# Eight second operands behind the weights of two MLP groups, and row sums that begin later: an FNet and MLP-Mixer kernel on one core

## The chip, the core and the metric

The kernel runs on one NeuronCore of a Trainium2 chip. The core has five engines with an instruction stream each. TensorE (PE in the profile) multiplies; its weight loads are shown as PEld. VectorE (DVE) does arithmetic on whole tiles, ScalarE (ACT) copies and activations, GpSimd (POOL) and SyncE (SP) mostly issue transfers here. Each engine works through its instructions strictly in the order in which they were written, and waits where an instruction needs something that another engine or a transfer has not finished. The metric is the device time of one execution, in microseconds; less is better.

## The reference

```python
def reference(A_x, A_dft_seq_re, A_dft_seq_im, A_dft_hid_re, A_dft_hid_im, B_x, B_w1, B_b1, B_w2, B_b2):
    x = A_x                                   # 1 x 2048 x 512, float32
    xn = _layernorm(x, axis=-1)
    # A: a = xn @ hid_re.T, b = xn @ hid_im.T   (2048 x 512)
    #    s = seq_re @ a - seq_im @ b                 (2048 x 2048 times 2048 x 512)
    s = _A_ref(xn, A_dft_seq_re, A_dft_seq_im, A_dft_hid_re, A_dft_hid_im)
    # B: y = layernorm(xn); h = gelu(y @ w1 + b1)  (2048 x 1792); h @ w2 + b2
    g = _silu(_B_ref(xn, B_w1, B_b1, B_w2, B_b2))
    return x + s * g
```

All inputs and the output are float32.

## The kernel before

Each float32 matrix product is made of three matmuls in a rounded format: an operand is split into a high part (ScalarE copies it rounded, `w1_round`, `y_round`, `a_round`) and a low part (VectorE subtracts the high part from the original, `w1_rest`, `y_rest`, `a_rest`), and high times high, high times low and low times high are added up in PSUM. On top of that the large products use a seven-product scheme for 2 x 2 blocks (Strassen's, in Winograd's form): sums of blocks are made first, seven block products follow instead of eight, and sums of the products give the result. So VectorE has to make, for every product, the sums as well as the low parts.

The program has four stages, each one long run of matmuls on TensorE.

1. **Hidden DFT, first half of the tokens** (`dft_mm`, line 338).
2. **Hidden DFT, second half** (`q_product`, `q_mm`, line 537): seven products in the order 1, 2, 5, 6, 3, 7, 4, each in four chunks c of six matmuls. Products 1, 6, 7 and 4 add into the same four PSUM banks one after the other. After product 6 ScalarE reads each bank (`q_after`, line 520), after product 7 VectorE reads it (line 525), and only then may product 4 add its own chunk to that bank.
3. **MLP, first layer** (`h_product`, line 657): seven groups j of weight columns, for each of them seven products in the order 1, 5, 6, 2, 3, 7, 4 (product 4 of one group comes after product 5 of the next). For groups 0 and 1 the tokens are taken in two halves (s): group 0 with the second half (`ONE`), group 1 with the second half, group 0 with the first half (`ZERO`), group 1 with the first half. A product of one half is six matmuls, of both halves twelve. The right operands are the normalised tokens and their sums: `11`, `t1`, `t2`, `21`, `22`, `t3`, `t4` for products 1, 5, 6, 2, 3, 7, 4, each once per half (in the profile `y_0h`, `yt_0l` and so on: a digit for the half, 0 is the first, then h or l for the part; a t marks the sums). `y_scale` (line 461) multiplies by the row of factors, `y_sum` (line 475) makes the sums in place. The left operands are the weights of the group: `w1_load` (line 433) fetches 512 KB, `w1_sums` (lines 437 to 440) makes four sums, `w1_round` (line 444) and `w1_rest` (line 83) split them. The weights have a single raw buffer, so the next load waits for `w1_rest` of the group before; the loads of groups 1 and 2 are issued by GpSimd, the others by SyncE. `h_after` moves products out of PSUM: ScalarE copies or applies GELU (lines 673 and 662), VectorE adds product 2 (line 702), product 3 (line 708) and product 7 (line 712). Product 4 adds into the bank that line 712 reads, so TensorE has to wait for line 712 before it.
4. **MLP, second layer** (`m_product`, line 838; products in the order 1, 4, 2, 5, 6, 3, 7 with seven units j each), and then the **sequence DFT** (line 838 too, then line 1156). In each unit of the second layer VectorE and ScalarE prepare operands three units ahead; SyncE loads them five ahead into seven buffers of a pool called `room`.

The sequence DFT needs sums of the hidden DFT's results. They are made by eight pieces of work, `extras[0]` to `extras[7]` (function `sums_a`), each in three steps: load two tiles of 512 KB (line 733), four VectorE operations (lines 737 to 740), store four results of 256 KB (line 744). Before the change pieces 0 to 4 run in groups 1 to 5 of the first layer and pieces 5, 6, 7 in products 5, 6 and 3 of the second layer. Their tiles come from the same `room` pool.

The order of all this is written out by hand: a table of `then(...)` steps that run between the chunks of `q_product`, and a table `y_late` of steps that run before a given product of the first layer. The order in the tables is the order in which VectorE and ScalarE get their instructions.

## Time and profile before

| what | value |
|---|---|
| time, median of 3 runs (lowest, highest) | 682.1 us (680.96, 682.46) |
| the profiled execution: its own time | 681.11 us |
| the profiled execution: span from first to last instruction | 679.3 us |
| TensorE busy | 664.6 us, 2908 matmuls |
| VectorE busy | 544.2 us, 592 instructions |
| ScalarE busy | 354.3 us, 395 instructions |
| moved by DMA | 172.28 MB, mean 254 GB/s |

The profile comes from one execution. Times inside it count from the span's start. A row of a timeline has the start, the duration, the engine, the line, the operation, the tiles written and read, how many instructions are merged into the row, and in brackets how long the engine was idle before it and what ended that. Instructions of one engine overlap a little, so the step from one start to the next is often shorter than the duration. A matmul of this kernel takes 0.39 us from start to end, while the next one starts 0.227 us later when nothing holds it up.

### The profile page before, as it was taken

To read this page: it belongs to the slowest core of one execution; us is meant where nothing else is said; L and a number is where in the kernel's file an instruction comes from. 1 tells how busy PE (TensorE), PEld (TensorE's weight loads), DVE (VectorE), ACT (ScalarE), POOL (GpSimd) and SP (SyncE) were. 2 spreads that over 40 slices of the span, in tenths; PEclk is the share of its full clock that TensorE was granted. 3 is DMA by queue.
4 is the path that set the end of the run, shared out by engine and by line. 5 is a ranking of instruction groups with operands and counts; after the bars stand their busy time and mean duration, and the time that the engine had idled before them with its cause. 6 is when DMAs were issued, how large, how long until landed. Compare 5 with 4: busy or idle time off the path is not lost.

```text
span 679.3 us, 8185 instructions
## 1 busy us (share of the span) xinstructions
PE 664.6 (98%) x2908; PEld 543.2 (80%) x2908; DVE 544.2 (80%) x592; ACT 354.3 (52%) x395; POOL 50.6 (7%) x84
## 2 busy tenths in 40 slices
PE   8999987999999999999999999999999999999997
PEld 5887875877888888888888888888888888888885
DVE  7998986487887775777997998729977389998985
ACT  4745664544445746656365654537445364646540
POOL 1001000122212110000000100000000001220100
PEclk9999998999999999999999999999999999999999
DMA  9778270398999998588899998415544548997983
GB/s 318 258 270 216 102 247 32 144 334 322 381 357 313 402 419 335 192 276 305 306 317 410 394 324 302 147 57 187 185 156 119 161 109 250 304 254 244 308 263 126
DMA packets 70329, 172.28 MB, mean 254 GB/s; under 512 B 6640, under 2 KB 21008, under 8 KB 70288
## 3 DMA queue, kind: packets, MB, share of 16 engines
q1 hardware_dynamic: 57904, 131.36, 54.8%
q0 software_dynamic: 12032, 39.86, 18.9%
q10 hardware_dynamic: 352, 0.54, 0.2%
q8 instruction: 23, 0.38, 0.2%
q14 instruction: 18, 0.15, 0.1%
HBM read 121.38 MB, written 50.35 MB: 253 GB/s over the span
## 4 chain that ended last, share of the span: by engine, by line
PE 84%; DVE 5%; issue 5%; DMA 2%; ACT 2%; POOL 1%; SPq 0%; POOLq 0%; DVEq 0%; ACTq 0%
PE pz L838 19%; PE px L838 18%; PE ma L838 11%; PE mb L838 8%; PE hy L657 8%; PE pd L338 6%; PE pw L838 5%; PE hz L657 3%; PE hx L657 2%; PE px L1156 2%; PE pw L1156 2%; POOL h_d L665 1%; DMA rw<-wt 1%; DVE xT L475 1%; DVE q L525 1%
## 5 line engine op out<-in xcount | busy, mean ns | idle before, releaser
L944 DVE TENSOR_TENSOR c<-c,c 128x1024 f32<-128x1024 f32 x32 | 39.0, 1220 | 4.1 <-DMA c<-ct 4.1
L662 ACT ACTIVATE hc<-hc,b_t 128x1024 f32<-128x1024 f32 (+1 forms) x18 | 17.3, 962 | 26.6 <-DVE hc L702 22.4
L65 DVE TENSOR_TENSOR R_b1l<-c,R_b1h 128x1024 fp32r<-128x1024 f32 x16 | 19.5, 1221 | 14.0 <-ACT R_b1h L64 10.7
L838 PE MATMUL pw<-R_s1h,L 128*128 128x512 f32 x96 | 29.7, 389 | 0.0
L64 ACT ACTIVATE R_s3h<-c 128x1024 fp32r<-128x1024 f32 x16 | 17.0, 1061 | 23.8 <-DVE c L944 12.4
L64 ACT ACTIVATE R_b2h<-c 128x1024 fp32r<-128x1024 f32 x16 | 16.9, 1058 | 21.6 <-DVE c L949 17.1
L65 DVE TENSOR_TENSOR R_s2l<-c,R_s2h 128x1024 fp32r<-128x1024 f32 x16 | 19.5, 1222 | 8.9 <-PE pz L838 8.9
L64 ACT ACTIVATE R_s2h<-c 128x1024 fp32r<-128x1024 f32 x16 | 17.0, 1061 | 16.7 <-PE px L838 9.3
L83 DVE TENSOR_TENSOR w1l<-w1r,w1h 128x1792 fp32r<-128x1792 f32 x7 | 14.2, 2023 | 13.1 <-ACT w1h L444 13.1
L65 DVE TENSOR_TENSOR R_s3l<-c,R_s3h 128x1024 fp32r<-128x1024 f32 x16 | 19.5, 1221 | 3.9 <-PE pz L838 3.8
L64 ACT ACTIVATE R_s1h<-c 128x1024 fp32r<-128x1024 f32 x16 | 16.4, 1051 | 11.6 <-DVE c L955 11.6
L64 ACT ACTIVATE R_b1h<-c 128x1024 fp32r<-128x1024 f32 x16 | 16.7, 1053 | 11.1 <-DMA c<-ct 5.1
L952 POOL DMA_DIRECT2D c<-ct x8 | 7.0, 875 | 201.5 <-issue 148.1
L64 ACT ACTIVATE R_a1h<-c 128x1024 fp32r<-128x1024 f32 x16 | 16.9, 1054 | 8.9 <-PE pz L838 7.2
L657 PE MATMUL hy<-yt_1h,w1h 128*128 128x512 f32 x42 | 17.1, 408 | 4.3 <-DVE hc L712 4.3
L838 PEld LDWEIGHTS pw<-R_s1h,L 128*128 128x128 f32 x96 | 18.0, 188 | 3.7
L65 DVE TENSOR_TENSOR R_b2l<-c,R_b2h 128x1024 fp32r<-128x1024 f32 x16 | 19.4, 1219 | 1.5 <-PE px L838 1.5
L65 DVE TENSOR_TENSOR R_a1l<-c,R_a1h 128x1024 fp32r<-128x1024 f32 x16 | 19.5, 1220 | 1.0 <-PE px L838 0.7
L65 DVE TENSOR_TENSOR R_s4l<-c,R_s4h 128x1024 fp32r<-128x1024 f32 x16 | 19.5, 1220 | 0.7 <-PE px L838 0.7
L64 ACT ACTIVATE w2h<-w 128x1024 fp32r<-128x1024 f32 (+1 forms) x14 | 13.2, 946 | 12.8 <-DVE w L770 3.9
L949 DVE TENSOR_TENSOR c<-c,c 128x1024 f32<-128x1024 f32 x16 | 19.6, 1223 | 0.4
L64 ACT ACTIVATE R_s4h<-c 128x1024 fp32r<-128x1024 f32 x16 | 16.8, 1052 | 5.3 <-PE pz L838 4.9
(950 smaller groups left out, 2221.9 us busy)
## 6 DMA issues: line engine op xcount, KB each, us to landing
c<-ct SPq DMA_DIRECT2D x68, 512.0 KB, 6.1
m<-h_d SPq DMA_DIRECT2D x48, 512.0 KB, 6.6
h_d<-ht POOLq DMA_DIRECT2D x21, 512.0 KB, 6.6
s_d<-sa SPq DMA_DIRECT2D x32, 256.0 KB, 4.0
la<-s_d SPq DMA_DIRECT2D x32, 256.0 KB, 6.2
h_d<-hc POOLq DMA_DIRECT2D x13, 512.0 KB, 4.8
x<-x SPq DMA_DIRECT2D x16, 256.0 KB, 4.9
sa<-a_d SPq DMA_DIRECT2D x8, 512.0 KB, 5.6
```

The costliest lines, as they stand in the source:

```text
L64: nc.scalar.activation(hi, src, AF.Copy)
L65: nc.vector.tensor_sub(lo, src, hi.bitcast(F32))
L83: nc.vector.tensor_sub(hi_lo[1], src, hi_lo[0].bitcast(F32))
L338: nc.tensor.matmul(acc, xt[i, k][px], weights[m * NK + k][pw], start=n == 0, stop=n == len(terms) - 1)
L475: nc.vector.tensor_sub(t, y_raw[a, tau], y_raw[b, tau])
L657: nc.tensor.matmul(acc[:, tau, :], w[:, W1_AT[p], k * P:(k + 1) * P], r[:, k, :], start=p in (1, 5, 2) and i == 0, stop=p in (2, 3, 4) and ...
L662: nc.scalar.activation(dst, src, AF.Gelu_apprx_tanh, bias=b1_t[:, row:row + 1])
L838: nc.tensor.matmul(acc[k][:, tau, :], a, c[:, tau, :], start=first and i == 0, stop=last and i == len(terms) - 1, skip_group_check=True)
L944: nc.vector.tensor_sub(t, t, raw)
L949: nc.vector.tensor_add(raw, raw, t)
L952: nc.gpsimd.dma_start(out=t, in_=ct[1, 1, n], accum_op=ALU.add)
L1156: nc.tensor.matmul(acc[KEY[name]][k][:, tau, :], a[k], c[:, tau, :], start=False, stop=u == us[-1] and i == 2, skip_group_check=True)
```

## The change

Three things move; no operation is added or removed, and no size changes.

In the second half of the hidden DFT and in groups 0 and 1 of the first layer, the steps of `w1` (sums, rounding, low parts and loads of groups 0 and 1) are written further ahead, and the steps that make the right operands of the first token half are written later: `11` and `t1` come behind the weights of group 0, `t2`, `21`, `22`, `t3` and `t4` are spread over both half groups of the second token half, and the end of `t4` falls into group 0's first token half. `w1_sums(2)` goes into the same table. The table `y_late` gets the token half as part of its key. Pieces 0 to 2 of the row sums run in groups 3 to 5, and pieces 3 and 4 in products 4 and 2 of the second layer.

```diff
--- before.py
+++ after.py
@@ -603,9 +603,9 @@
     a_rest(5)
     y_rest("t1", 1)
     q_product(1, [then(y_scale, 1, 3), then(y_round, "22", 1)], [then(y_sum, "t2", 1)],
-              [then(y_round, "t2", 1), then(y_rest, "22", 1)], [then(y_rest, "t2", 1), then(a_round, 6)])
-    q_product(2, [post(2, 0), then(a_rest, 6)], [post(2, 1), then(y_sum, "t3", 1)],
-              [post(2, 2), then(y_round, "t3", 1), then(a_round, 3)], [post(2, 3)])
+              [then(y_round, "t2", 1), then(y_rest, "22", 1)], [then(a_round, 6)])
+    q_product(2, [post(2, 0), then(y_rest, "t2", 1)], [post(2, 1), then(a_rest, 6)],
+              [post(2, 2), then(y_sum, "t3", 1), then(y_round, "t3", 1), then(a_round, 3)], [post(2, 3)])
     q_product(5, [then(a_rest, 3)], [then(y_rest, "t3", 1), then(y_sum, "t4", 1), then(a_round, 7)],
               [then(y_round, "t4", 1), then(a_rest, 7)], [then(y_rest, "t4", 1)])
     early.close()
@@ -613,14 +613,12 @@
     wp = early.enter_context(tc.tile_pool(name="wp", bufs=4, reuse_waits="tile"))
     lp = early.enter_context(tc.tile_pool(name="lpm", bufs=2, reuse_waits="tile"))
     w1_load(0)
-    q_product(6, [then(y_scale, 0, 0), then(y_round, "11", 0)], [then(y_scale, 0, 1)],
-              [then(y_rest, "11", 0), then(y_sum, "t1", 0)], [then(y_round, "t1", 0)])
-    q_product(3, [post(3, 0), then(y_rest, "t1", 0)], [post(3, 1), then(w1_sums, 0)], [then(w1_round, 0), post(3, 2)],
-              [post(3, 3)])
-    q_product(7, [post(7, 0)], [post(7, 1), then(w1_rest, 0), then(w1_load, 1)], [post(7, 2)],
-              [post(7, 3), then(y_scale, 1, 1)])
-    q_product(4, [then(y_sum, "t2", 0), then(y_round, "t2", 0)], [then(y_rest, "t2", 0)], [then(w1_sums, 1)],
-              [then(y_scale, 1, 0)])
+    q_product(6, [then(y_scale, 0, 0)], [then(w1_sums, 0)], [then(w1_round, 0), then(y_scale, 0, 1)], [then(w1_rest, 0), then(w1_load, 1)])
+    q_product(3, [post(3, 0), then(y_round, "11", 0)], [post(3, 1), then(y_scale, 1, 1)], [post(3, 2), then(y_rest, "11", 0)],
+              [post(3, 3), then(y_sum, "t1", 0)])
+    q_product(7, [post(7, 0), then(y_round, "t1", 0)], [post(7, 1), then(w1_sums, 1)], [post(7, 2), then(y_rest, "t1", 0)],
+              [post(7, 3), then(w1_round, 1)])
+    q_product(4, [then(w1_rest, 1), then(w1_load, 2)], [then(y_sum, "t2", 0)], [], [then(y_scale, 1, 0)])
 
     rows_ps.close()
     yp = ctx.enter_context(tc.tile_pool(name="yp", bufs=4, space=bass.MemoryType.PSUM, reuse_waits="tile"))
@@ -791,12 +789,17 @@
         h_seq += [(j, p, s, done) for p in (1, 5)] + ([(last[0], 4, last[1], None)] if last else [])
         h_seq += [(j, p, s, done) for p in (6, 2, 3, 7)]
         last = j, s
-    y_late = {(0, 5): [then(w1_round, 1)],
-              (0, 6): [then(y_round, "21", 0), then(y_rest, "21", 0), then(w1_rest, 1), then(w1_load, 2)],
-              (0, 2): [then(y_round, "22", 0)],
-              (0, 3): [then(y_rest, "22", 0), then(y_sum, "t3", 0), then(y_round, "t3", 0)],
-              (0, 7): [then(y_rest, "t3", 0), then(y_sum, "t4", 0)],
-              (1, 1): [then(y_round, "t4", 0), then(y_rest, "t4", 0)]}
+    y_late = {(0, 5, 1): [then(y_round, "t2", 0)],
+              (0, 6, 1): [then(y_rest, "t2", 0)],
+              (0, 3, 1): [then(y_round, "21", 0)],
+              (0, 7, 1): [then(y_rest, "21", 0)],
+              (1, 5, 1): [then(y_round, "22", 0)],
+              (1, 6, 1): [then(y_rest, "22", 0), then(y_sum, "t3", 0)],
+              (1, 2, 1): [then(y_round, "t3", 0)],
+              (1, 3, 1): [then(y_rest, "t3", 0), then(w1_sums, 2)],
+              (1, 7, 1): [then(y_sum, "t4", 0)],
+              (0, 5, 0): [then(y_round, "t4", 0)],
+              (0, 6, 0): [then(y_rest, "t4", 0)]}
 
 
     m_order = [1, 4, 2, 5, 6, 3, 7]
@@ -995,7 +998,7 @@
             w2_load(1, 1)
 
     for j, p, s, done in h_seq:
-        for o in y_late.get((j, p), ()) if s == ONE else ():
+        for o in y_late.get((j, p, s.start), ()):
             o()
         h_product(j, p, s)
         if j == NJ - 1:
@@ -1009,12 +1012,13 @@
         if stores:
             store()
         if p == 4 and s.start == 0 and j + 2 < NJ:
-            w1_sums(j + 2)
+            if j:
+                w1_sums(j + 2)
             w1_split(j + 2)
             if j + 3 < NJ:
                 w1_load(j + 3)
-        if 0 < j < NJ - 1 and s.start == 0 and p in (1, 2, 3):
-            extras[j - 1][{1: 0, 2: 1, 3: 2}[p]]()
+        if 2 < j < NJ - 1 and p in (1, 2, 3):
+            extras[j - 3][{1: 0, 2: 1, 3: 2}[p]]()
 
     for u, (p, j) in enumerate(m_units):
         m_ahead("load", u + (6 if u < 2 else 5))
@@ -1053,8 +1057,8 @@
                 w2_split(nxt, 1)
         if j == 1 and p in (4, 2):
             w2_load(0, 1) if p == 4 else w2_load(1, 0)
-        if p in (5, 6, 3) and j in (0, 2, 4):
-            extras[{5: 5, 6: 6, 3: 7}[p]][j // 2]()
+        if p in (4, 2, 5, 6, 3) and j in (0, 2, 4):
+            extras[{4: 3, 2: 4, 5: 5, 6: 6, 3: 7}[p]][j // 2]()
         if (p, j) == (7, NJ - 1):
             m_evacuate(7)
         if p == 7:
```

Three places show what that does to the order. First VectorE at the end of the hidden DFT. `q5_` with `qy` are its reads after product 7 (line 525), `w1r0` and `w1r1` the raw weights of groups 0 and 1. Before:

```order
L525 SCALAR_TENSOR_TENSOR q5_0_792<-qy0_694,nq_89,q5_0_792 128x512
L525 SCALAR_TENSOR_TENSOR q5_0_792<-qy1_707,nq_89,q5_0_792 128x512
L83 TENSOR_TENSOR w1l0_911<-w1r0_841,w1h0_910 128x1792
L525 SCALAR_TENSOR_TENSOR q5_2_815<-qy2_716,nq_89,q5_2_815 128x512
L525 SCALAR_TENSOR_TENSOR q5_2_815<-qy3_729,nq_89,q5_2_815 128x512
L461 TENSOR_TENSOR xT1_1_237<-xT1_1_237,rowR_0_674 128x1024
L475 TENSOR_TENSOR xT0_0_676<-xT1_1_237,xT0_0_676 128x1024
L83 TENSOR_TENSOR yt2_0l_970<-xT0_0_676,yt2_0h_969 128x1024
L437 TENSOR_TENSOR w1r1_940<-w1r1_940 128x256
L438 TENSOR_TENSOR w1r1_940<-w1r1_940 128x256
L439 TENSOR_TENSOR w1r1_940<-w1r1_940 128x256
L440 TENSOR_TENSOR w1r1_940<-w1r1_940 128x256
```

And now:

```order
L83 TENSOR_TENSOR w1l0_872<-w1r0_841,w1h0_871 128x1792
L525 SCALAR_TENSOR_TENSOR q6_0_849<-qz0_785,qq_88,q6_0_849 128x512
L525 SCALAR_TENSOR_TENSOR q6_0_849<-qz1_795,qq_88,q6_0_849 128x512
L461 TENSOR_TENSOR xT1_1_237<-xT1_1_237,rowR_0_674 128x1024
L525 SCALAR_TENSOR_TENSOR q6_2_869<-qz2_808,qq_88,q6_2_869 128x512
L83 TENSOR_TENSOR y11_0l_894<-xT0_0_676,y11_0h_893 128x1024
L525 SCALAR_TENSOR_TENSOR q6_2_869<-qz3_821,qq_88,q6_2_869 128x512
L475 TENSOR_TENSOR xT0_0_676<-xT1_0_235,xT0_0_676 128x1024
L525 SCALAR_TENSOR_TENSOR q5_0_792<-qy0_694,nq_89,q5_0_792 128x512
L525 SCALAR_TENSOR_TENSOR q5_0_792<-qy1_707,nq_89,q5_0_792 128x512
L437 TENSOR_TENSOR w1r1_883<-w1r1_883 128x256
L438 TENSOR_TENSOR w1r1_883<-w1r1_883 128x256
```

The low part of group 0's weights now stands in front of the last reads after product 3 and of all reads after product 7, and the first two operands of the first token half (`y11_0`, `yt1_0`) stand between them; the sum `t2` is behind them.

Second VectorE in the first two half groups of the first layer. `hc50` and `hc51` are where the results of product 7 go for groups 0 and 1 (line 712 before, 710 now). Before, up to group 0's:

```order
L83 TENSOR_TENSOR y21_0l_1080<-xT0_1_680,y21_0h_1079 128x1024
L83 TENSOR_TENSOR w1l1_1067<-w1r1_940,w1h1_1066 128x1792
L702 TENSOR_TENSOR hc10_1063<-hc10_1063,hx0_1098 128x512
L83 TENSOR_TENSOR y22_0l_1096<-xT1_1_237,y22_0h_1095 128x1024
L475 TENSOR_TENSOR xT1_0_235<-xT1_1_237,xT1_0_235 128x1024
L708 TENSOR_TENSOR hu20_1092<-hu20_1092,hz0_1069 128x512
L83 TENSOR_TENSOR yt3_0l_1111<-xT1_0_235,yt3_0h_1110 128x1024
L475 TENSOR_TENSOR xT0_0_676<-xT0_1_680,xT0_0_676 128x1024
L712 TENSOR_TENSOR hc50_1076<-hc50_1076,hy0_1056 128x512
```

Now, up to group 0's, and then up to group 1's:

```order
L461 TENSOR_TENSOR xT0_1_680<-xT0_1_680,rowR_0_674 128x1024
L83 TENSOR_TENSOR yt2_0l_1069<-xT0_0_676,yt2_0h_1068 128x1024
L700 TENSOR_TENSOR hc10_1065<-hc10_1065,hx0_1091 128x512
L706 TENSOR_TENSOR hu20_1088<-hu20_1088,hz0_1071 128x512
L83 TENSOR_TENSOR y21_0l_1102<-xT0_1_680,y21_0h_1101 128x1024
L710 TENSOR_TENSOR hc50_1078<-hc50_1078,hy0_1058 128x512
```

```order
L700 TENSOR_TENSOR hc11_1128<-hc11_1128,hx1_1163 128x512
L83 TENSOR_TENSOR yt3_0l_1161<-xT1_0_235,yt3_0h_1160 128x1024
L437 TENSOR_TENSOR w1r2_976<-w1r2_976 128x256
L438 TENSOR_TENSOR w1r2_976<-w1r2_976 128x256
L439 TENSOR_TENSOR w1r2_976<-w1r2_976 128x256
L440 TENSOR_TENSOR w1r2_976<-w1r2_976 128x256
L706 TENSOR_TENSOR hu21_1158<-hu21_1158,hz1_1133 128x512
L475 TENSOR_TENSOR xT0_0_676<-xT0_1_680,xT0_0_676 128x1024
L710 TENSOR_TENSOR hc51_1140<-hc51_1140,hy1_1121 128x512
```

Before, four operations on operands (`y22_0l`, two sums, `yt3_0l`) stand between line 702 and line 712 beside line 708; now one does between lines 700 and 710, `y21_0l`, beside line 706. Ahead of group 1's line 710 there are now a low part, the four weight sums of group 2 and a sum, which before were done earlier or, for the weight sums, later.

Third SyncE in the second layer, ahead of the loads of the weights `w221`, which the sum for product 5 needs in product 2 (line 770). `m16` and its like are operands of that layer, `sa` the tiles of the row sums, `s1_d3` and its like the stored results of piece 3. Before:

```order
L812 DMA m16_2301<-h2_d2_1016 128x1024
L812 DMA m17_2323<-h2_d3_1017 128x1024
L812 DMA m18_2341<-h2_d4_1018 128x1024
L812 DMA m19_2363<-h2_d5_1019 128x1024
L763 DMA w221_0_2383<-w2 128x1024
L763 DMA w221_1_2384<-w2 128x768
```

And now:

```order
L742 DMA s1_d3_144<-sa1_3_2199 256x1x256
L742 DMA s3_d3_160<-sa0_3_2197 256x1x256
L742 DMA s2_d3_152<-sa0_3_2197 256x1x256
L742 DMA s4_d3_168<-sa1_3_2199 256x1x256
L815 DMA m16_2289<-h2_d2_1018 128x1024
L815 DMA m17_2311<-h2_d3_1019 128x1024
L815 DMA m18_2329<-h2_d4_1020 128x1024
L731 DMA sa0_4_2351<-a_d4_129 128x2x512
L731 DMA sa1_4_2353<-b_d4_137 128x2x512
L815 DMA m19_2355<-h2_d5_1021 128x1024
L761 DMA w221_0_2375<-w2 128x1024
L761 DMA w221_1_2376<-w2 128x768
```

The four stores of piece 3 and both loads of piece 4 are now in front of these weights; in product 4 the loads of piece 3 stand in the same way in front of the weights `w212` for product 2.

## The prediction

> **What bounds the kernel now.** I read the page's head first, then who TensorE waits for, then TensorE's timeline around its waits.
>
> ```profile
> span 679.3 us, 8185 instructions
> PE 664.6 (98%) x2908; PEld 543.2 (80%) x2908; DVE 544.2 (80%) x592; ACT 354.3 (52%) x395; POOL 50.6 (7%) x84
> ...
> PE hy L657 <- DVE hc L712: 5.7, 3, 4.3
> PE hy L657 <- ACT q L520: 1.8, 1, 1.8
> ```
>
> TensorE is busy 98% of the span, so only its gaps can be won. By far the largest two lie at the first layer: three waits for VectorE's line 712, 5.7 us together and 4.3 us the longest, and one of 1.8 us for ScalarE's reads after product 4 of the hidden DFT. TensorE's timeline shows where, and what follows:
>
> ```profile
> 92.12 0.39 PE L537 MATMUL qy<-W,yt_1l 128*128 128x512 f32 x1
> 94.27 0.50 PE L657 MATMUL hy<-y_1h,w1h 128*128 128x512 f32 x1 [1.76 <-ACT q L520]
> ...
> 105.07 0.39 PE L657 MATMUL hz<-yt_1h,w1l 128*128 128x512 f32 x1
> 109.78 0.70 PE L657 MATMUL hy<-yt_1h,w1h 128*128 128x512 f32 x1 [4.32 <-DVE hc L712]
> ...
> 114.22 0.39 PE L657 MATMUL hx<-y_1h,w1h 128*128 128x512 f32 x1
> ...
> 162.84 0.50 PE L657 MATMUL hy<-yt_0h,w1h 128*128 128x512 f32 x1 [1.18 <-DVE hc L712]
> 110.00:115.00 5.00, 5.00 (x16) 3.93 (x16) 1.23 (x1) 3.61 (x6) 0.00 (x0) 0.67 0.00 0
> ```
>
> The last row is a window of 5 us; the 0.67 in it is the granted clock. A matmul takes 0.227 us from start to start, so six (a product of one token half, "a six" below) take 1.36 us. From 105.07 the next matmul was due at 105.30 and came at 109.78: 4.48 us lost. After that wait the clock is down, and the twelve matmuls from 109.78 to 114.22 took 4.44 us where 2.72 were due, 1.72 us more. From 114.22 to 162.84 TensorE does 34 sixes (17 to the end of group 1, 13 in group 2, 4 in group 3), worth 46.24 us, in 48.62: another 2.38 us lost in small pieces.
>
> Why line 712 was late is seen on VectorE:
>
> ```profile
> 102.69 0.68 DVE L702 TENSOR_TENSOR hc<-hc,hx 128x512 f32<-128x512 f32 x1
> ...
> 106.77 1.23 DVE L83 TENSOR_TENSOR yt_0l<-xT,yt_0h 128x1024 fp32r<-128x1024 f32 x1 [0.53 <-ACT yt_0h L79]
> 107.91 1.22 DVE L475 TENSOR_TENSOR xT<-xT,xT 128x1024 f32<-128x1024 f32 x1
> 109.04 0.68 DVE L712 TENSOR_TENSOR hc<-hc,hy 128x512 f32<-128x512 f32 x1
> ```
>
> VectorE works without a pause that matters, on operands of the first token half that are not wanted yet, while TensorE waits for the one read at the end of the list.
>
> **The change, part by part.** The sums below are against the profiled execution, 681.11 us (span 679.3 and 1.8 around it). It lies 1.0 under the median of 682.1.
>
> *End of the hidden DFT.* The same work stands in another order, and product 4 of the DFT waits for VectorE's reads after product 7. The rows for the price:
>
> ```profile
> 74.91 2.35 DVE L461 TENSOR_TENSOR xT<-xT,rowR 128x1024 f32<-128x1024 f32 x2
> 77.25 1.23 DVE L83 TENSOR_TENSOR y_0l<-xT,y_0h 128x1024 fp32r<-128x1024 f32 x1
> ...
> 82.67 0.42 DVE L437 TENSOR_TENSOR w1r<-w1r 128x256 f32<-128x256 f32 x1
> ...
> 84.13 1.40 DVE L525 SCALAR_TENSOR_TENSOR q<-qz,qq,q 128x512 f32<-128x512 f32 x2
> 85.45 1.40 DVE L525 SCALAR_TENSOR_TENSOR q<-qy,nq,q 128x512 f32<-128x512 f32 x2
> 86.77 2.01 DVE L83 TENSOR_TENSOR w1l<-w1r,w1h 128x1792 fp32r<-128x1792 f32 x1
> 88.70 1.40 DVE L525 SCALAR_TENSOR_TENSOR q<-qy,nq,q 128x512 f32<-128x512 f32 x2
> 84.30 1.71 ACT L444 ACTIVATE w1h<-w1r 128x1792 fp32r<-128x1792 f32 x1 [3.46 <-DVE w1r L440]
> 92.59 1.06 ACT L79 ACTIVATE yt_0h<-xT 128x1024 fp32r<-128x1024 f32 x1 [3.43 <-DVE xT L475]
> 93.55 1.83 ACT L520 ACTIVATE q<-qy,nq 128x512 f32<-128x512 f32 x3
> 86.91 0.61 PE L537 MATMUL qy<-W,yt_1h 128*128 128x512 f32 x2
> DMA to landing us min/median/max: 3.6/4.8/6.8
> ```
>
> Both orders are alike up to 74.91. From start to start: an operation on 128 x 1024 steps 1.14 to 1.17 us, four weight sums 1.46 (82.67 to 84.13), a read 0.66, a low part of weights 1.93. Now: one scaling to 76.1, four sums to 77.5, another scaling to 78.7. ScalarE rounds the weights from 77.7 to 79.4, so VectorE pauses 0.7 and makes the low part from 79.4 to 81.4. Two reads to 82.7, scaling 83.8, read 84.5, low part 85.7, read 86.3, sum 87.5. The first read after product 7 ends at 88.2 instead of about 86.1; product 4 (24 matmuls, 5.44 us) begins then and not at 86.91. Second read 88.8; the sums of group 1's weights 90.3 (their load, issued by GpSimd once the low part is done at 81.4, lands by 88.2 or so even with the last row's longest 6.8); third read 91.0, when the third chunk is due; a low part to 92.1; fourth read 92.8, 0.4 late. The product ends at 94.2, not 92.35.
>
> What made ScalarE late is gone in return: the rounding of `t2`, ahead of which ScalarE idled 3.43 us for the sum, is no longer between the reads of product 4. ScalarE rounds group 1's weights from 90.3 to 92.0 and reads the first two chunks by 93.2 (0.6 each, from the row at 93.55). The first layer starts at **94.2 against 94.27**: one wait takes the place of the other, worth -0.1 us. Bounds: without the late reads ScalarE still sets 93.2 (-1.1). If the load of group 1 took 10.6 us, the longest of the other 512 KB loads below, the sums would begin at 92.3, 3.5 late (+3.4, and +5.1 with a clock drop like the one above). Since VectorE's list is fixed and the load has time, I take -0.1.
>
> *First two half groups.* Group 1's weights are done at 94.8, ahead of need. `yt2_0l` waits for ScalarE to 97.5 and ends at 98.7. Product 2, the fourth six, ends at about 99.9; line 700 follows at once, line 706 at 101.3; ScalarE's high part of `21` (1.06, as in the row at 92.59) ends at 102.4, then come `y21_0l` and line 710, which runs from 103.6 to 104.3. Product 4 of group 0, eight sixes after 94.2, is due at 105.1: it no longer waits, with 0.8 us to spare. That is **-4.48, and -1.72** for the clock. What is late next is group 1: line 700 ends at 110.1; then `yt3_0l` (1.14), the weight sums of group 2 (1.46), line 706 (0.6), the sum `t4` (1.14) and line 710 (0.69) end at 115.1. TensorE's product 4 there, 15 sixes after 94.2, is due at 114.6: a new wait of **+0.5**. The operands of the first half are ready some 8 us or more before use (`t4` at 116.2, used at 124.6). On GpSimd nothing stands behind the earlier loads of weights until the first layer's first stores.
>
> *The row sums leave groups 1 and 2.* A row of VectorE shows what they cost there, another the landing of their loads:
>
> ```profile
> 157.66 0.69 DVE L737 TENSOR_TENSOR sa<-sa,sa 128x512 f32<-128x512 f32 x1 [2.95 <-DMA sa<-b_d]
> DMA to landing us min/median/max: 3.6/6.3/10.6
> ```
>
> In group 2 VectorE sat 2.95 us behind a tile that had not landed, with lines 708 and 712 queued behind it, and TensorE waited at 162.84. Of the 2.38 us lost from 114.22 to 162.84 I take **-2.1** as won (bounds 0 and -2.4). Groups 3 to 5 carry one piece each as before, and the first of them is loaded a group early. The next fence has windows of groups 3 to 6 and of products 4 and 2 of the second layer, rows of VectorE and SyncE there, and two rows of the table of transfers (size, median us to landing):
>
> ```profile
> 163.00:234.00 71.00, 71.00 (x314) 58.77 (x315) 54.46 (x59) 38.86 (x36) 14.34 (x27) 1.00 0.94 347
> 255.00:274.00 19.00, 19.00 (x85) 15.76 (x84) 10.13 (x9) 10.70 (x12) 0.00 (x0) 1.00 0.90 343
> 274.00:293.00 19.00, 19.00 (x85) 15.72 (x85) 14.32 (x13) 10.38 (x12) 0.00 (x0) 1.00 0.57 197
> 281.24 2.09 DVE L770 TENSOR_TENSOR w<-w,w 128x1024 f32<-128x1024 f32 x2
> 283.25 1.22 DVE L822 TENSOR_TENSOR M19l<-m,M19h 128x1024 fp32r<-128x1024 f32 x1
> 300.02 0.68 DVE L737 TENSOR_TENSOR sa<-sa,sa 128x512 f32<-128x512 f32 x1
> ...
> 302.80 1.22 DVE L822 TENSOR_TENSOR M26l<-m,M26h 128x1024 fp32r<-128x1024 f32 x1
> 258.80 1.22 DVE L822 TENSOR_TENSOR M11l<-m,M11h 128x1024 fp32r<-128x1024 f32 x1
> 261.70 1.07 SPq L763 DMA_DIRECT2D w<-w  x2
> w<-w SPq DMA_DIRECT2D x4, 384.0 KB, 9.5
> s_d<-sa SPq DMA_DIRECT2D x32, 256.0 KB, 4.0
> ```
>
> TensorE lost nothing in those groups (71.00 of 71).
>
> *Products 4 and 2 of the second layer* (windows 255 and 274) get a piece each: VectorE 2.8 us (300.02 to 302.80 in product 5, which has one already) on 10.1 and 14.3 of 19. Tightest is product 2: `M19l` would end at 283.25 + 2.8 + 1.2 = 287.3, and its unit, the sixth of 2.72 us from 274.66, is due at 288.3. In SyncE's queue the weights `w221` now wait for four stores and two loads. Piece 3's operations follow `M11l`, from 260 to 262.8; its stores go out behind them and have landed some 4 us later, which frees the last buffers that the six loads ahead of `w221` need: `w221` goes out at about 269 (before, 261.7). With 9.5 us to land, the median of such loads, it is there at 278.5, needed at 281.24. I cost this at **0**, hidden by the operands' lead of three units.
>
> The Trainium skill speaks against that ("DMA: Bandwidth & Descriptors", "Issuing engines are not separate DMA queues"): transfers from all engines end on the same 16 DMA engines, so 2 MB more compete with everything. An estimate from it: 2 MB in 19 us are 110 GB/s on top of 343, which took a share of 0.90; full share would be 381, so 3 to 4 us of transfers spill into product 2, which has room (0.57). `w221` would land at about 282, within the slack of 1.0; the sum stays.
>
> *Sum*: -0.1 - 4.48 - 1.72 + 0.5 - 2.1 = -7.9. The profiled execution would take 673.2, the median 1.0 more: **674.2 us**.
>
> **The rivals.** (a) VectorE's list in the half groups is later than I add up, by some 2 to 3 us: both product 4s wait again. For it: every step there hangs on ScalarE and a slack of only 0.8. Against it: five operations fewer stand ahead of line 710. Waits of about 2.5 leave -5.4: 676.7. (b) The wait moves into the hidden DFT: the late load of group 1, +5.1 with the clock, leaves about -2.8: 679.3. Against it: 7.1 us in hand where 6.8 was the longest. The Trainium skill ("TensorE: Matmul & The Clock Gate", Part 1) halves the clock after an idle window of about 3.4 us: the rows agree, 4.32 us idle brought it and 1.76 did not, and by the rule a wait of 3.5 stands on the edge, which would make it 679.3 or 677.6. (c) Slower: SyncE stands so long behind the stores and buffers of pieces 3 and 4 that `w221` lands late. VectorE's line 770 then stops all its later work. It decides from a landing at 288.4: 7.2 after 281.2, less the slack of 1.0, is a wait of 6.2, 1.7 more for the clock, and the gain of 7.9 is gone; with a landing at 292 it is 685.7. For it: the queue is in order and now waits there for stores. Against it: products 5, 6 and 3 run so already, though their weights are loaded by then. (d) No change: the first layer is held by its transfers (0.94 share in groups 3 to 6), and what TensorE gains is waited for there: 682. Against it: TensorE does not wait in that window, and 4 MB have left the groups ahead of it.
>
> **How the numbers follow.** Forecast 0.62, (a) 0.17, (b) 0.08, (c) 0.06, (d) 0.07. Around 674.2 the forecast's own ends are 672.5 (the start at 93.2, all of 2.38 won) and 676; (a) takes the range to 678.5, which leaves out (b), (c) and (d), about 2 in 10. About 0.2% is what the measurement can tell from no change: faster 0.87, same 0.06, slower 0.07.
>
> **What would show it.** Right: the wait at 105 for line 712's successor gone, no window at clock 0.67 there; a wait of 1 to 2 us inside product 4 of the hidden DFT for VectorE's reads; a short one near 114.6; product 4 of group 2 at about 155 instead of 162.84; no wait of TensorE from there to the end. Wrong: TensorE waits for line 710 for more than 2 us, a wait at the weight sums of group 1, or one in products 2 and 5 of the second layer behind line 768's landing.

## The result

| | median | lowest to highest | profiled execution: time, span |
|---|---|---|---|
| before | 681.75 us | 680.96 to 682.46 | 681.11, 679.3 |
| after | 672.83 us | 672.27 to 673.93 | 673.93, 672.2 |

The changed kernel takes 0.9871 of the time before, with an interval of 0.9854 to 0.9889: 8.9 us less. The forecast was 674.2, with 672.5 to 678.5 around it.

The head of the page after, and all that TensorE waits for longer than 0.2 us behind the start-up:

```profile
span 672.2 us, 8165 instructions
PE 663.4 (99%) x2908; PEld 544.5 (81%) x2908; DVE 544.0 (81%) x592; ACT 355.1 (53%) x395; POOL 50.7 (8%) x84
...
PE qy L537 <- DVE q L525: 1.8, 1, 1.8
PE hy L655 <- DVE hc L710: 0.3, 1, 0.3
```

The three waits of 5.7 us for VectorE's last addition of a group (line 712 before, 710 now) are one of 0.3. The wait of 1.8 us for ScalarE behind the hidden DFT is gone, and one of 1.8 us for VectorE's reads inside the DFT has come. TensorE's timeline after the change gives the borders of the stages:

```profile
53.13 0.62 PE L537 MATMUL qy<-W,y_1h 128*128 128x512 f32 x2
...
87.71 0.73 PE L537 MATMUL qy<-W,yt_1h 128*128 128x512 f32 x2 [1.78 <-DVE q L525]
...
94.93 0.39 PE L655 MATMUL hy<-y_1h,w1h 128*128 128x512 f32 x1
...
115.77 0.50 PE L655 MATMUL hy<-yt_1h,w1h 128*128 128x512 f32 x1 [0.28 <-DVE hc L710]
...
226.08 0.39 PE L841 MATMUL ma<-M0h,w2h 128*128 128x512 f32 x1
...
666.50 0.39 PE L1160 MATMUL px<-R_b1h,L 128*128 128x512 f32 x1
```

The starts of this DFT stage, of the first and of the second layer, and of the last matmul were read in the same way from the timeline of each kernel below. All times are of its profiled execution, from start to start, in us; "before" starts its DFT at 53.61, its first layer at 94.27, its second at 233.69 and its last matmul at 674.11. A ratio is to the kernel before as it was run beside that kernel (medians of 681.08 to 681.75), so kernels of different rows are compared by it.

| kernel | this DFT stage | first layer | second layer to last matmul | median, ratio to before |
|---|---|---|---|---|
| before | 40.66 | 139.42 | 440.42 | 681.75 |
| after | 41.80 | 131.15 | 440.42 | 672.83, 0.9871 |
| after, once more | 40.65 | 131.15 | 440.41 | 673.61, 0.9891 |
| e1 row sums alone | 40.67 | 137.13 | 440.41 | 679.93, 0.9980 |
| e2 row sums back | 41.78 | 132.70 | 440.41 | 675.18, 0.9915 |
| e3 list packed | 40.66 | 133.44 | 440.43 | 675.50, 0.9927 |
| e4 reads first | 38.08 | 131.92 | 440.41 | 671.38, 0.9854 |
| e5 group 1 freed | 41.76 | 130.56 | 440.42 | 673.51, 0.9879 |
| e6 = e4 + e5 | 38.08 | 131.32 | 440.42 | 671.30, 0.9846 |
| e7 two pieces | 41.76 | 131.14 | 447.57 | 681.33, 0.9996 |
| f1 shorter wait | 40.77 | 131.13 | 440.42 | 672.66, 0.9869 |
| f2 longer wait | 42.89 | 131.14 | 440.41 | 675.89, 0.9916 |
| f3 three edits | 38.08 | 130.56 | 440.41 | 669.99, 0.9828 |
| f4 other queue | 40.65 | 131.16 | 444.49 | 677.35, 0.9942 |

From before to after the first layer gave 8.27 us, the DFT stage took 1.14, the second layer moved by nothing. The rest (the stages ahead are 0.48 shorter, what follows the last matmul is about 0.5 longer) is of the size in which two executions of one kernel differ: the DFT starts anywhere from 52.71 to 53.89 in the kernels above, whose work ahead of it is the same.

All three columns of times have a floor. The DFT's 168 matmuls at 0.22667 us are 38.08, the first layer's 576 are 130.56, and the 1943 from the second layer to the last matmul are 440.41. Whatever a kernel has above that is waiting or a lower clock.

In the profile after, the product behind the new wait took 7.22 us (87.71 to 94.93) instead of 5.44, without another wait in it: the granted clock was half for 3.4 us, which by itself costs 1.7. In the other profile of the same kernel the clock stayed full, and the stage took 1.15 us less. Which waits bring the clock down is the last section's matter; "the drop" below means this.

### The profile page after: what moved, and what is told of

Same layout as the page of the kernel before. It is cut to its first block, busy times and chain, and to the rows that moved or that the text cites. A ratio compares the mean times of both kernels' runs of the same rounds, so it can differ in the third digit from the quotient of the medians.

```text
span 672.2 us, 8165 instructions
## 1 busy us (share of the span) xinstructions
PE 663.4 (99%) x2908; PEld 544.5 (81%) x2908; DVE 544.0 (81%) x592; ACT 355.1 (53%) x395; POOL 50.7 (8%) x84
## 4 chain that ended last, share of the span: by engine, by line
PE 93%; DVE 4%; ACT 1%; issue 1%; DMA 0%; DVEq 0%; ACTq 0%
PE pz L841 19%; PE px L841 18%; PE ma L841 11%; PE hy L655 11%; PE mb L841 8%; PE pd L338 6%; PE hz L655 5%; PE pw L841 5%; PE hx L655 3%; PE px L1160 2%; PE pw L1160 2%; PE qy L537 1%; PE pd L353 1%; DVE q L525 1%; DVE xT L475 1%
## 5 line engine op out<-in xcount | busy, mean ns | idle before, releaser
L65 DVE TENSOR_TENSOR R_s1l<-c,R_s1h 128x1024 fp32r<-128x1024 f32 x16 | 18.8, 1219 | 0.1
```

Source lines behind the costliest of these rows:

```text
L65: nc.vector.tensor_sub(lo, src, hi.bitcast(F32))
```

## The experiments

### e1: the row sums alone

Kernel before, with only this:

```diff
-        if 0 < j < NJ - 1 and s.start == 0 and p in (1, 2, 3):
-            extras[j - 1][{1: 0, 2: 1, 3: 2}[p]]()
+        if 2 < j < NJ - 1 and p in (1, 2, 3):
+            extras[j - 3][{1: 0, 2: 1, 3: 2}[p]]()
...
-        if p in (5, 6, 3) and j in (0, 2, 4):
-            extras[{5: 5, 6: 6, 3: 7}[p]][j // 2]()
+        if p in (4, 2, 5, 6, 3) and j in (0, 2, 4):
+            extras[{4: 3, 2: 4, 5: 5, 6: 6, 3: 7}[p]][j // 2]()
```

> Only one part of the change on the kernel before: the row sums for the sequence DFT run in groups 3 to 5 and in products 4 and 2 of the second layer; the weights and the operand list stand where they stood before. Theory (terms D and F): the 2.1 us that PE lost in groups 1 and 2 to VectorE's row sums go and nothing comes back later, so 681.75 - 2.1 = 679.6, with the wait of 4.5 us at product 4 of group 0 unchanged and no wait of PE over 0.3 us between 240 and 300. Rival: the stalls move with the row sums into groups 3 to 5 or to the second layer, 681.7 or more.

Measured: 679.93 against 681.08 beside it, ratio 0.9980 (0.9966 to 0.9993). The median gave 1.15 us, with an interval that reaches from 0.5 to 2.3; the trace says 139.42 - 137.13 = 2.29 for the first layer, and its waits are:

```profile
PE hy L657 <- DVE hc L712: 4.3, 1, 4.3
PE hy L657 <- ACT q L520: 1.7, 1, 1.7
```

Of the three waits for line 712 the large one is left, as the theory said, and the second layer took no longer.

### e2: the row sums back

The changed kernel with the two edits of e1 taken back.

> The changed kernel with the row sums put back into groups 1 and 2 (and products 5, 6, 3); the weights' and operands' new places stay. Theory: 672.83 + 2.1 = 674.9, the loss shows as waits of h matmuls for VectorE's evacuations in groups 1 and 2, one of about 2 us behind the load of a row piece. Rival: the loss in groups 1 and 2 came from the late operand list being worked off there together with the row sums, and with the weights ahead it does not come back: 672.8 to 673.3. Either way the wait ahead of the DFT's product 4 stays at 1.8 us; its clock is open: if the drop to about half speed behind that wait belongs to the wait, it is here again (product 4 takes about 7.2 us), and if it came by chance product 4 takes 5.4 to 5.6.

Measured: 675.18, ratio 0.9915 (0.9896 to 0.9935). The loss is back, 1.55 us in the first layer, where the theory had 2.1. VectorE's row shows the same cause as before the change, the load that had not landed:

```profile
151.34 0.69 DVE L735 TENSOR_TENSOR sa<-sa,sa 128x512 f32<-128x512 f32 x1 [3.15 <-DMA sa<-b_d]
```

So by the profiles moving the row sums is worth 1.6 to 2.3 us, depending on the order around them, and the rival of no loss falls. Product 4 of the DFT had the lower clock here (stage 41.78), as the table of waits in the last section has it.

### e3: the operand list packed

```diff
-              (0, 6, 1): [then(y_rest, "t2", 0)],
-              (0, 3, 1): [then(y_round, "21", 0)],
-              (0, 7, 1): [then(y_rest, "21", 0)],
-              (1, 5, 1): [then(y_round, "22", 0)],
...
+              (0, 6, 1): [then(y_rest, "t2", 0), then(y_round, "21", 0), then(y_rest, "21", 0)],
+              (0, 2, 1): [then(y_round, "22", 0)],
+              (0, 3, 1): [then(y_rest, "22", 0), then(y_sum, "t3", 0), then(y_round, "t3", 0)],
+              (0, 7, 1): [then(y_rest, "t3", 0), then(y_sum, "t4", 0)],
+              (1, 1, 1): [then(y_round, "t4", 0), then(y_rest, "t4", 0)],
+              (1, 3, 1): [then(w1_sums, 2)]}
```

> The changed kernel with the operand list packed as before into the second half of group 0 (rest of t2 and of 21, round and rest of 22, sum, round and rest of t3 and the sum t4 all ahead of its last evacuation), with the weights of groups 0 and 1 still ahead. Theory (the list, and not the weights alone, made the wait): VectorE has four operations of 1.15 us more than now ahead of the last evacuation of group 0 and had 2.3 us idle there, so that the evacuation ends at about 107.1 instead of 104.8 where PE is due at about 105.7: a wait of about 1.5 us at product 4 of group 0, with 0 to 1.7 us of lower clock behind it, and the 0.44 us wait of group 1 gone: 672.83 + 1.1 to 2.8 = 673.9 to 675.6. Rival: it was the weights of group 1 (2.0 us of VectorE, 1.7 of ScalarE) in that half that made the wait, and spreading the list was not needed: 672.4 to 672.9.

Measured: 675.50, ratio 0.9927 (0.9900 to 0.9954), inside the theory's range and outside the rival's. TensorE's timeline:

```profile
106.99 0.50 PE L655 MATMUL hy<-yt_1h,w1h 128*128 128x512 f32 x1 [1.76 <-DVE hc L710]
109.17 0.50 PE L655 MATMUL hy<-yt_1h,w1h 128*128 128x512 f32 x1 [0.51 <-ACT hc L671]
```

The wait at product 4 of group 0 is back, 1.76 us of the 4.32, and ScalarE is late once behind it. Above the floor of 130.56 the first layer had 8.86 before, 6.57 in e1 (row sums moved), 2.88 here (weights ahead as well) and 0.59 in the changed kernel (list spread as well). Weights ahead are worth 3.7, spreading 2.3, in this order. The 3.7 holds the 1.7 us of lower clock that e1 still had behind its long wait and that the profiled execution of e3 had not.

### e7: a second piece of row sums in product 2

```diff
-        if p in (4, 2, 5, 6, 3) and j in (0, 2, 4):
-            extras[{4: 3, 2: 4, 5: 5, 6: 6, 3: 7}[p]][j // 2]()
+        if p in (2, 5, 6, 3) and j in (0, 2, 4):
+            for i in {2: (3, 4), 5: (5,), 6: (6,), 3: (7,)}[p]:
+                extras[i][j // 2]()
```

> The changed kernel with the row-sum piece of the second layer's product 4 moved into product 2 beside that product's own: two pieces are loaded, added and stored there. It measures the cover of term F. Theory: VectorE is free 1.0 us ahead of PE there (the split of the 20th operand ends at 279.64, due 280.65); a second piece adds 2.9 us, so PE waits 1.9 us once, with 0 to 1.7 us of lower clock behind it: 674.7 to 676.4. Rival (the third rival of the prediction, transfers): the weights of the next product are late behind four loads and eight stores, and PE waits at the first matmul of product 5 instead, for the weight split. Rival two: VectorE can put off its other work, no wait, 672.8.

Measured: 681.33, ratio 0.9996 (0.9980 to 1.0012). One piece too many in one product eats the whole gain of the change: 7.15 us in the second layer, four times the first wait. TensorE, then SyncE's queue and ScalarE:

```profile
282.91 0.50 PE L841 MATMUL ma<-M19l,w2h 128*128 128x512 f32 x1 [1.61 <-DVE M19l L825]
295.71 0.51 PE L841 MATMUL mb<-M23h,w2h 128*128 128x512 f32 x1 [1.85 <-ACT M23h L819]
296.97 0.80 PE L841 MATMUL mb<-M23l,w2h 128*128 128x512 f32 x1 [0.76 <-DVE M23l L825]
...
270.77 12.43 SPq L815 DMA_DIRECT2D m<-h_d  x3
283.25 6.63 SPq L742 DMA_DIRECT2D s_d<-sa  x8
289.98 1.56 SPq L815 DMA_DIRECT2D m<-h_d  x3
...
294.60 1.06 ACT L819 ACTIVATE M23h<-m 128x1024 fp32r<-128x1024 f32 x1 [6.77 <-DMA m<-h_d]
```

The first wait came where the theory put it and was nearly as long (1.61, with 1.76 lost, where 1.9 was said). What no theory had is the second: the load of the 23rd operand stands behind eight stores in SyncE's queue, 6.6 us of issues, goes out at 289.98, right behind the last of them, and lands at 294.6. The stores themselves had stood behind three loads that took SyncE until 283.20. Then the clock halves (0.50 from 296.7 on). The rival named the queue but had the wrong transfer behind it.

### f4: the same two pieces, their stores in another queue

```diff
-                nc.sync.dma_start(out=s_d[q, i].rearrange("p (c e) -> p c e", c=2), in_=t[m][:, :, e * W2:(e + 1) * W2])
+                (nc.gpsimd if i in (3, 4) else nc.sync).dma_start(
+                    out=s_d[q, i].rearrange("p (c e) -> p c e", c=2), in_=t[m][:, :, e * W2:(e + 1) * W2])
```

> The kernel with two pieces in product 2, with the eight stores of these two pieces issued on GpSimd's queue instead of SyncE's. It parts the 7.2 us that the second piece cost. Theory: VectorE's part is the first wait alone (1.6 us), and the 23rd operand came late since its load stood behind eight stores in SyncE's queue (6.6 us of issues); with the stores elsewhere only the wait of 1.6 us is left, short enough to leave the clock alone: before's time less 6, 674.5 to 675. Rival: the load waited for a buffer that the row pieces hold, then the second wait of 1.85 us and its clock stay: 679 to 681.

Measured: 677.35, ratio 0.9942 (0.9922 to 0.9962), between the two. The stores on GpSimd, two rows of ScalarE, and what TensorE waited for:

```profile
275.13 5.67 POOL L742 DMA_DIRECT2D s_d<-sa  x8 [35.75 <-DMA m<-h_d]
...
287.80 1.06 ACT L820 ACTIVATE M23h<-m 128x1024 fp32r<-128x1024 f32 x1 [1.59 <-DMA m<-h_d]
298.83 1.06 ACT L820 ACTIVATE M26h<-m 128x1024 fp32r<-128x1024 f32 x1 [5.21 <-DMA m<-h_d]
...
PE ma L842 <- DVE M19l L826: 1.6, 1, 1.6
PE mb L842 <- DVE M26l L826: 0.8, 1, 0.8
PE mb L842 <- DVE M40l L826: 0.7, 1, 0.7
```

Counted from the start of the second layer (224.60 here, 226.52 in e7), the 23rd operand lands 4.9 us sooner than in e7, 63.20 against 68.08, and its wait is gone with its clock. In e7 its load went out as soon as the last store had been issued, so there the queue held it and it did not wait for a buffer of its own. But the edit does more than shorten SyncE's queue: GpSimd issues the stores from 275.13 on, where SyncE came to them at 283.25, so the buffers of the row pieces come free sooner as well. What f4 shows is that the stores' place in SyncE's queue made the second wait; how much of it was the time of the issues and how much buffers that came free late, it does not part.

The Trainium skill ("DMA: Bandwidth & Descriptors", "Issuing engines are not separate DMA queues") calls what another issuing engine saves usually small beside the transfer; here eight issues took SyncE 6.6 us.

But two waits of 0.8 and 0.7 came behind the row sums of later products, and the second layer is still 4.07 above before's 440.42 where 1.6 was expected. For the 26th low part the row at 298.83 names what was late: its load, for which ScalarE sat idle 5.21 us. Ahead of the 40th, VectorE works without a pause from the 37th low part on (325.79), and that one had waited for a load too (ScalarE idle 4.57 us before 324.69). The transfers' share was 1.02 from 292 to 312. That late loads are behind the 40th is argued from these rows; no run here takes them away.

### After, once more

> The changed kernel once more, unaltered, beside the three that follow. Expected 672.8 in the median. Its profile is a second look at the clock in product 4 of the hidden DFT: theory one, the wait of 1.8 us takes the clock down each time (product 4 takes about 7.2 us again); theory two, it does so only in some executions (5.4 to 5.6 us here, and the time of this execution about 1.7 us shorter than the first one's 673.93).

Measured: 673.61, ratio 0.9891 (0.9873 to 0.9909). The profile shows the second theory right (stage 40.65, no drop), and the last section says why: a border of the clock's grid, at 86.90, cut the wait. Its numbers were not met: product 4 took 6.07 us (88.47 to 94.54) instead of 5.4 to 5.6, in part since a wait of 0.3 for VectorE's fourth read follows where the clock stays full, and this execution is only 0.4 us shorter than the first one, since the stages ahead of the DFT took 0.76 longer.

### e4: VectorE's reads first

```diff
-    q_product(3, [post(3, 0), then(y_round, "11", 0)], [post(3, 1), then(y_scale, 1, 1)], [post(3, 2), then(y_rest, "11", 0)],
-              [post(3, 3), then(y_sum, "t1", 0)])
-    q_product(7, [post(7, 0), then(y_round, "t1", 0)], [post(7, 1), then(w1_sums, 1)], [post(7, 2), then(y_rest, "t1", 0)],
-              [post(7, 3), then(w1_round, 1)])
-    q_product(4, [then(w1_rest, 1), then(w1_load, 2)], [then(y_sum, "t2", 0)], [], [then(y_scale, 1, 0)])
+    q_product(3, [post(3, 0), then(y_round, "11", 0)], [post(3, 1)], [post(3, 2)], [post(3, 3)])
+    q_product(7, [post(7, 0)], [post(7, 1), then(y_rest, "11", 0)], [post(7, 2)], [post(7, 3)])
+    q_product(4, [then(w1_sums, 1)], [then(w1_round, 1), then(y_scale, 1, 1), then(y_sum, "t1", 0)], [then(w1_rest, 1), then(w1_load, 2)],
+              [then(y_round, "t1", 0), then(y_rest, "t1", 0), then(y_sum, "t2", 0)])
...
-              (0, 3, 1): [then(y_round, "21", 0)],
-              (0, 7, 1): [then(y_rest, "21", 0)],
+              (0, 3, 1): [then(y_scale, 1, 0), then(y_round, "21", 0)],
+              (1, 1, 1): [then(y_rest, "21", 0)],
```

> The changed kernel with VectorE's four reads of the DFT's product 7 put ahead of the scale, the sums and the residual that delayed them (scale of 22, sum t1, the sums and residual of group 1's weights come behind the reads; the scale of 21 goes to the half of group 0). Theory (term A): the wait of 1.8 us at product 4 goes and with it whatever clock it cost, so product 4 starts at about 85.8 instead of 87.7 and the first layer at about 91.3 instead of 94.9 in the profile: 672.83 - 1.9 = 670.9 without a change of clock, down to 669.2 if the median execution had lost 1.7 us of clock. Rival: what was put off makes group 0 wait instead (its last evacuation ends about 1 us ahead of PE now), 671.5 to 672.8; or the first layer's start hangs on ScalarE's reads of product 4 and gains less than 1 us.

Measured: 671.38, ratio 0.9854 (0.9836 to 0.9872), 2.2 below the unaltered kernel beside it. VectorE's reads and TensorE:

```profile
83.70 1.40 DVE L525 SCALAR_TENSOR_TENSOR q<-qy,nq,q 128x512 f32<-128x512 f32 x2
86.14 1.40 DVE L525 SCALAR_TENSOR_TENSOR q<-qy,nq,q 128x512 f32<-128x512 f32 x2
...
97.47 0.50 PE L654 MATMUL hz<-y_1h,w1h 128*128 128x512 f32 x1 [0.47 <-ACT hc L670]
```

The DFT stage is at its floor, 38.08. A short wait for ScalarE's copy (line 670, 671 in the changed kernel) comes in group 0, a part of what the rival feared, and the first layer takes 0.77 us longer. So the wait at product 4, and with it 2.6 us of the DFT stage, was a matter of VectorE's order and not of a transfer.

### e5: group 1 freed, and e6: both

```diff
-              (1, 3, 1): [then(y_rest, "t3", 0), then(w1_sums, 2)],
-              (1, 7, 1): [then(y_sum, "t4", 0)],
+              (1, 3, 1): [then(y_rest, "t3", 0)],
+              (0, 1, 0): [then(y_sum, "t4", 0), then(w1_sums, 2)],
```

> The changed kernel with the sums of group 2's weights and the sum t4 moved behind the last evacuation of group 1's first half. Theory (term C): VectorE has 2.6 us less ahead of that evacuation, the wait of 0.44 us goes and nothing else moves: 672.4. Rival: the weights of group 2 then come late at its first product, or t4 at product 4 of the second half of group 0: 672.8 or more.

Measured: 673.51, ratio 0.9879 (0.9863 to 0.9895). The first layer is at its floor of 130.56, 0.59 less than without this edit. The median cannot tell it from the unaltered kernel's 673.61: executions with and without the drop of the clock lie further apart than the gain.

> Both of the two edits before: the reads of the DFT's product 7 first, and group 1's last evacuation freed. Theory: the two gains add up, 672.83 - 1.9 - 0.4 = 670.5, down to 668.8 with the clock. Rival: one of them eats the other since the work put off meets in groups 0 and 1: 671 to 672.5.

Measured: 671.30, ratio 0.9846 (0.9829 to 0.9863). The median lies in the rival's range. By the profile neither gain eats the other: the first layer again gains 0.60 (131.92 to 131.32), and what keeps it 0.76 above its floor is the wait for ScalarE's copy that e4 brought. By the medians, e6 and e4 are equal within the spread.

### f1 and f2: the wait made shorter and longer

f1 moves `post(3, 3)` behind `post(7, 1)`; f2 moves `y_scale(1, 0)` from the end of product 4 to the last step ahead of `post(7, 0)`.

> The changed kernel with one read moved: VectorE's last read of the DFT's product 3 goes behind the second read of product 7, so that the wait ahead of product 4 is 0.66 us shorter (1.1 instead of 1.78), while the fourth read of product 7, for which product 4 waits later anyway, comes when it came. What it tells apart is the clock. Theory (the clock is set on a fixed grid of 3.413 us: half speed in the next period when PE stood idle for more than about 1.75 us of one): a wait of 1.1 us never brings it, so product 4 runs at full clock in the profile, the stage from the DFT's first product to the first layer takes 40.65 us as in the undisturbed executions of the changed kernel, no execution is granted less than 0.997 in the mean, and the median is that of the changed kernel's executions without the drop, 0.989 of before, 0.5 us below the mixed median. Rival (any wait here may bring it down, by chance): half speed is seen in about half of the executions, as in the changed kernel.

Measured: 672.66 (672.46 to 673.05), ratio 0.9869 (0.9855 to 0.9882). The wait was 1.24 us where 1.1 was expected, the stage 40.77, the clock full, and the four executions lie within 0.6 us, where those of the unaltered kernel beside the other runs lay within 2.5. The median came below the 0.989 of the theory; the unaltered kernel was not run beside it.

> The changed kernel with the scale of 21 (1.13 us of VectorE) ahead of the reads of product 7 instead of behind them: the wait ahead of product 4 grows from 1.78 to 2.9 us. Theory (the grid of 3.413 us, half speed after more than about 1.75 us idle within one period): a wait of 2.9 us escapes only where a boundary of the grid cuts it into two pieces that are both under 1.75, which is (1.75 - 1.15)/3.41 = 18% of the places; so most executions have the drop, the DFT stage takes about 42.9 us, and the median is 1.1 us of wait and about 0.5 us of more frequent drops above the changed kernel: 0.991 to 0.992 of before. Rival (the drop comes by chance, whatever the length between 1.6 and 2.9): it is seen no more often than before and the median rises by 1.1 us alone.

Measured: 675.89 (675.18 to 676.45), ratio 0.9916 (0.9902 to 0.9929), in the middle of what the grid gives. The interval reaches into what the rival gives as well (1.1 us above the unaltered kernel's 0.9871 and 0.9891), so the median does not decide between them, and one profile does not show how often the drop comes. In that profile the stage took 42.89, and the clock was half from 90.24 on:

```profile
90.00:91.00 1.00, 1.00 (x5) 0.62 0.91 340
91.00:92.00 1.00, 1.00 (x4) 0.50 0.49 184
```

### f3: three edits together

e6, and `then(y_round, "t2", 0)` goes from product 5 of group 0 to product 6, its low part from product 6 to product 2.

> The two edits together (reads of product 7 first, group 1 freed) and the rounding of t2 moved behind ScalarE's copy of product 5, which it held up (PE waited 0.47 us for that copy). Theory: no wait of PE over 0.2 us is left between the hidden DFT and the second layer, the first layer takes 130.6 us instead of 131.3: 0.6 us below the kernel with the two edits, 0.984 of before. Rival: the residual of t2, which now comes later, makes the next evacuations of group 0 late, and nothing is gained.

Measured: 669.99 (669.27 to 670.51), ratio 0.9828 (0.9815 to 0.9842). TensorE has no wait from the start of this DFT stage to the last matmul; all three stretches are at their floors:

```profile
86.04 0.61 PE L537 MATMUL qy<-W,yt_1h 128*128 128x512 f32 x2
...
91.48 0.39 PE L654 MATMUL hy<-y_1h,w1h 128*128 128x512 f32 x1
```

This is faster than both kernels: by the medians 11.5 us less than before beside it, and with 0.9828 of before against the change's 0.9871 and 0.9891 some 3 to 4 us less than the change. From the start of this DFT stage to the last matmul nothing is left to win by order alone.

## Why the prediction was right, step by step

**End of the hidden DFT: -0.1 forecast.** One wait did take the place of the other, and the stage is equal in an execution without the drop (40.66 before, 40.65 in the changed kernel once more). VectorE in the profile after:

```profile
85.12 0.74 DVE L525 SCALAR_TENSOR_TENSOR q<-qz,qq,q 128x512 f32<-128x512 f32 x1
85.78 1.21 DVE L475 TENSOR_TENSOR xT<-xT,xT 128x1024 f32<-128x1024 f32 x1
86.92 1.40 DVE L525 SCALAR_TENSOR_TENSOR q<-qy,nq,q 128x512 f32<-128x512 f32 x2
88.24 0.41 DVE L437 TENSOR_TENSOR w1r<-w1r 128x256 f32<-128x256 f32 x1
...
91.49 0.74 DVE L525 SCALAR_TENSOR_TENSOR q<-qy,nq,q 128x512 f32<-128x512 f32 x1
```

The sequence is the forecast one, and the sums of group 1's weights (88.24) did not wait for their load. What failed is what the prediction made of the clock. It says "4.32 us idle brought it and 1.76 did not" and charges the new wait no lower clock, but this wait of 1.78 did bring it: the first layer began at 94.93 (95.41 on the clock of before, as the DFT began 0.48 sooner), not 94.2. The 1.76 of before had a border of the grid inside it, so that only 1.43 of it fell into one period. The forecast is off there by 1.15 us in some executions and by nothing in others.

**First two half groups: -4.48, -1.72, then +0.5.** Line 710 of group 0 ran from 104.14 to 104.82 (forecast 103.6 to 104.3), ahead of TensorE. In group 1 it came late, 0.44 us at 115.77 (forecast 0.5 at 114.6); all that this wait cost is the 0.59 of e5. With the row sums taken out by e1, this step is 6.57 - 0.59 = 5.98, against 5.7 forecast.

**Row sums out of groups 1 and 2: -2.1.** 2.29 by e1, 1.55 by e2. Taken together the first layer gave 8.27 where the two steps said 7.8. Product 4 of group 2 began at 155.36, where about 155 was forecast.

**Products 4 and 2 of the second layer: 0.** 440.42 before and after. The rows of the changed kernel (VectorE, TensorE, SyncE):

```profile
278.42 1.22 DVE L825 TENSOR_TENSOR M19l<-m,M19h 128x1024 fp32r<-128x1024 f32 x1
...
280.71 0.39 PE L841 MATMUL ma<-M19l,w2h 128*128 128x512 f32 x1
...
261.46 1.16 SPq L761 DMA_DIRECT2D w<-w  x2
```

The low part ends at 279.64, 1.07 us ahead of its matmul; forecast was a slack of 1.0. `w221` goes out at 261.46, which is 269.1 on the clock of before (the second layer starts 7.61 sooner), as forecast. The transfers spilled from product 4 into product 2 as the prediction estimated: their share was 0.99 and 0.79 in the two (247.4 to 266.4 and 266.4 to 285.4), where 0.90 and 0.57 had stood, and TensorE was busy 19.00 of 19 us in each. That the step was worth 0 hung on that one microsecond: e7 shows what the next piece costs.

**The rivals.** (a), the list later: no wait of 2.5 us anywhere; in e3, with the list packed, one of 1.76 comes. (b), the wait moves into the DFT: not by the load, which was in time, but the drop it reckoned with came behind a wait half as long. (c), SyncE's queue: not in this change; in e7 the queue is overfilled, and with the stores taken out of it (f4) 3.1 of the 7.15 us come back. (d), transfers hold the first layer: TensorE waits for no transfer there.

The median came 1.4 us below the forecast: the sum of the steps, -7.9, was short by 0.5 in the first layer, and the step from the profiled execution to the median (+1.0) did not hold for the changed kernel, whose profiled execution was its slowest (673.93): it had the drop, and its mean granted clock was 0.995 against 0.998 and 0.999 in the other three. That the number came this near is in part luck: by the profiled execution, 673.93 against 673.2, the drop that was not reckoned with made the forecast too low, by the median it is too high. The lower end of the range, 672.5, is not what its two terms give either: 674.2 less 1.0 (a start at 93.2) and 0.28 (all of 2.38) is 672.9, and the measured median lies just below that.

## What to carry to other kernels

Put an engine's reads of a finished accumulator ahead of its preparations, and spread preparations up to their own due time; a list that is packed "early" makes late whatever stands at its end. Reckon a wait of TensorE by what follows it as well: here more than about 1.75 us inside one period of 3.41 us halved the clock for the next period, so a wait of 1.8 cost 1.15 more in one execution and nothing in another, and one of 1.24 cost only itself. Before work is hidden in a stage, count its slack and the queue behind it: with 1.0 us of slack one piece was free, and the next cost 7.2.
